# Order of the steps at the seam between attention and experts: shared rows, the first unit's transposes, GpSimd weight sums

## The chip, the cores and the metric

The kernel runs on one core of a Trainium2 chip. The metric is the device time of one execution in microseconds (us); what is compared is the median of several runs. The engines are TensorE (PE in the profile, with its weight loads as PEld), VectorE (DVE), ScalarE (ACT), GpSimd (POOL) and SyncE (SP, which only issues transfers). Each engine works through its own queue in order, and an instruction that waits holds everything behind it.

## The reference, cut to what matters

```python
# attention: batch 8, heads 8, seq 576, head_dim 64; half of the heads see a plain window of 32,
# half a window of 128 with dilation 4
scores = scale * np.matmul(q, k.transpose(0, 1, 3, 2))
scores = np.where(masks[None, :, :, :], scores, -1000000000.0)
attn = softmax(scores)
x = (attn @ v) rearranged to (B, S, H * D)          # 8 x 576 x 512

# experts: 8 of them, w1[e] 512 x 1024, w2[e] 1024 x 512
for b in range(B):
    for s in range(S):
        fresh_e = int(np.argmax(logits[b, s]))
        e = fresh_e if s == 0 or local_gate[b, s] < 0.5 else prev_e
        prev_e = e
        h = np.maximum(x[b, s] @ w1[e], 0.0)
        out[b, s] = p[e] * (h @ w2[e])
```

Each token goes through one expert. Which one depends on its own logits or on the token before it, so the routing is a running scan over the sequence. Everything is computed in float32.

## The kernel before, in words

**Attention.** The 64 heads (8 batches of 8) are worked on two at a time, in 32 pairs. The loop over `n` (lines 1016 to 1044) does `scores(n)`, then `values(n - 1)`, and in every second iteration `turn`, which transposes a finished half of a batch's columns on TensorE, and `store`, which writes it to a buffer in DRAM (`xd`). `load(n + 3)` fetches the keys, queries and values of a later pair through SP's queue. The values tile `vt` has 96 rows for each block of 64 queries: 64 rows of the block and 32 rows that it shares with the block before. The shared rows are copied by GpSimd from the rest of the tile (line 247), directly after the load of the same pair is issued, three iterations ahead of `scores` of that pair.

**Routing.** After every fourth `turn`, `route(g)` puts the routing of 1152 tokens into the list `waiting`: `logits`, `fresh`, `carry`, `carry_over`, `carry_in`, `choose`, `gate`, `place`, `lanes_of`, four `matrices`, `products`, and for groups 1 and 3 `count`, `table` and the tokens. Each step is a few small instructions on TensorE, VectorE and ScalarE. `gap` takes steps from the list in the attention loop by a budget, and `work_gap` takes one after each product of the experts.

**Experts.** The tokens of an expert are gathered into units. A unit of kind "pair" has 256 rows. Units 0 and 1 are chosen early, from the first half of the tokens, while attention still runs. Units 2 and on follow when all tokens are routed. For a unit, `rows_of` gathers rows from `xd` by indirect DMA on GpSimd's queue (line 797); in the attention loop the eight gathers of units 0 and 1 are taken from `rows`, one an iteration, after `load(n + 3)`. `features` transposes them on TensorE (line 812), ScalarE copies them to `xe` (line 813), and VectorE makes four sums `xc` of them.

A pair's two matrix products are each done as seven products of half size instead of eight (`chain`), with sums of the quarters of both operands before and additions after. `hidden(u)` needs `sums[0]`, the four sums of the quarters of w1 (`sums_left`, lines 766 to 769, 128x1024 each), and `xc`. `output(u)` needs `sums[1]`, the four sums of w2 (`sums_right`, lines 772 to 775), and `hc`, four sums of the hidden values (lines 766 to 769 again, 128x512). Product 0 and product 3 use no sums; products 1, 2, 4 and 5 use one left sum each, in order, and products 1, 2, 4 and 6 one right sum. `sums[0]` exists once, so a sum for the next unit can be written when the product that reads the old one is done; so it is with `sums[1]`. In the hidden step VectorE adds a product to an earlier one (line 891), and product 6 waits for the second of these additions. In the output step VectorE does so too (line 965), and `send` writes each half of the unit's rows to the output by indirect DMA on GpSimd's queue (line 909).

TensorE, VectorE and GpSimd execute in the order of the program text. `soon` is a list of sums that `work_gap` puts between products, one or two after each product, and while `waiting` is not empty only when its length is odd. `flush` issues the rest, and `now` issues a list at once. At the seam the order is: hidden step of unit 0 with the w2 sums of unit 0 between; two hc sums; transposes of unit 1; two hc sums and the xc sums of unit 1; output step of unit 0 with the w1 sums of unit 1 between; hidden step of unit 1 with its w2 sums between; four hc sums; output step of unit 1, after whose fourth product `feed` loads weights, transposes unit 2 and gathers unit 3; hidden step of unit 2; transposes of unit 3; w1 sums of unit 3; hidden step of unit 3. From there on the output step of a unit follows the hidden step of the next one.

Of the kernel before, what the change touches and what calls it, by code (L numbers as in the profile page):

```python
# [192 lines left out]
def whole(ctx, tc, exact, bad, qk, v, wgl, w1, w2, con, msk, qmk, out, cst, wg, ones):  # L193
# [50 lines left out]
    def load_values(n):  # L244
        vt = vts[n % AHEAD]
        nc.sync.dma_start(out=vt[WIN:].rearrange("p u i e -> p (u i e)"), in_=v[n])
        nc.gpsimd.tensor_copy(vt[:WIN, :, 1:], vt[QB:, :, :NB - 1])  # L247

    def load(n):
# [134 lines left out]
    def logits(g):  # L384

        st = routes[g]
        xt = st["xt"]
        lp = bank([P, NQ], "lp")
        for kk in range(DK):
            for c in range(NC):  # L390
                if kk < CH:
                    rhs = xt[:, 0, c * NQ:(c + 1) * NQ, kk]
                else:
                    b, s = divmod(c * NQ, S)
                    rhs = xt[:, 1, b * S:(b + 1) * S, kk - CH].rearrange("p (c j) -> p j c", c=DIL)
                    rhs = rhs[:, s // DIL:(s + NQ) // DIL]
                nc.tensor.matmul(lp[c * LW:(c + 1) * LW], lhsT=wg[:, kk], rhs=rhs,
                                 start=(kk == 0), stop=(kk == DK - 1), skip_group_check=True,
                                 tile_position=(0, c * LW))
        st["le"] = le = sm.tile([P, NQ], F32, name="le")  # L400
        nc.scalar.copy(le, lp)
# [332 lines left out]
    def gap(add=None):  # L734
        if add is not None:
            credit[0] = min(credit[0] + add, add)
        alone = False
        while waiting and not alone and (add is None or credit[0] >= 0):
            f, cost, _ = waiting.pop(0)
            credit[0] -= cost  # L740
            if f:
                f()
            alone = add is None or not waiting or waiting[0][2]

    def work_gap(sums=True):
        if waiting:
            gap()
            sums = sums and len(waiting) % 2
        for _ in range(len(soon) > 4 and 2 or len(soon) > 0 if sums else 0):
            soon.pop(0)()  # L750

    def now(push):
        for f in push:
            f()

    def flush():
        while soon:
            soon.pop(0)()

    def quarter(w, i, k, second):  # L760
        if second:
            return w[:, FK // 2 * i:FK // 2 * (i + 1), D // 2 * k:D // 2 * (k + 1)]
        return w[:, FK // 2 * i:FK // 2 * (i + 1), DK // 2 * k:DK // 2 * (k + 1)]

    def sums_left(to, a11, a12, a21, a22):
        return [lambda: nc.vector.tensor_tensor(to[:, 0], a21, a22, op=Alu.add),  # L766
                lambda: nc.vector.tensor_tensor(to[:, 1], to[:, 0], a11, op=Alu.subtract),
                lambda: nc.vector.tensor_tensor(to[:, 2], a11, a21, op=Alu.subtract),
                lambda: nc.vector.tensor_tensor(to[:, 3], a12, to[:, 1], op=Alu.subtract)]

    def sums_right(to, b11, b12, b21, b22):
        return [lambda: nc.vector.tensor_tensor(to[:, 0], b12, b11, op=Alu.subtract),
                lambda: nc.vector.tensor_tensor(to[:, 1], b22, to[:, 0], op=Alu.subtract),
                lambda: nc.vector.tensor_tensor(to[:, 2], b22, b12, op=Alu.subtract),
                lambda: nc.vector.tensor_tensor(to[:, 3], b21, to[:, 1], op=Alu.subtract)]

    def sums_of_weights(u, second):

        i = units[u]["slot"]
        assert (u, second) in loads  # L780
        if second:
            return sums_right(sums[1], *(quarter(raw2[i], k, j, True) for k in range(2) for j in range(2)))
        return sums_left(sums[0], *(quarter(raw1[i], f, k, False) for f in range(2) for k in range(2)))

    xg, xe, xc, ht = {}, {}, {}, {}

# [189 lines left out]
    def route(g, slow):  # L976
        steps = [(logits, 0, True), (fresh, 3.0, True), (carry, 1.0, True), (carry_over, 0.5, True), (carry_in, 0.5, True),
                 (choose, 1.5, True), (gate, 1.5, False), (place, 0.5, True), (lanes_of, 1.3, False)]
        if slow:
            waiting.insert(0, (lambda: logits(g), 0, True))  # L980
            steps.pop(0)
        for f, *how in steps:
            waiting.append((lambda f=f: f(g), *how))
            if slow and f == fresh:
                waiting.append(pause)
        waiting.extend((f, cost, False) for f, cost in zip(matrices(g), (0.9, 0.9, 0.9, 1.7)))
        if g in (EARLY - 1, NG - 1):
            late = g == NG - 1
            counts = count(late)
            steps = [(lambda: next(counts), 1.8, True)] * (PASSES + 1 if exact and late else 2)  # L990
            waiting.append(steps.pop())
            waiting.append((lambda: products(g, False), 0.3, True))
            waiting.extend(steps)
            waiting.append(pause)
            waiting.append((lambda: table(late), 0.3, True))
            if late:
                waiting.append((late_tokens, 1.5, True))
            else:
                waiting.append((early_tokens, 1.5, True))
                waiting.append((early_weights, 0, False))  # L1000
        else:
            waiting.append(pause)
            waiting.append((lambda: products(g, not g), 0.3, True))
# [12 lines left out]
    for n in range(NPB + 2):  # L1016
        if n < NPB:
            (scores_exact if exact else scores)(n)
        gap(SHARE)
        if 1 <= n <= NPB:  # L1020
            values(n - 1)
        if n == NPB - 4:
            soon.extend(sums_of_weights(0, False))
        if soon:
            soon.pop(0)()
        if n >= 3 and n % 2 == 1:
            turn((n - 3) // 2)
            if (n - 3) // 2 % (2 * GB) == 2 * GB - 1:
                route((n - 3) // 2 // (2 * GB), n == NPB + 1)
        gap(SHARE)  # L1030
        if n + 3 < NPB:
            load(n + 3)
        if n >= 3 and n % 2 == 1:
            store((n - 3) // 2)
        if n in (4, 6, 8, 10):
            load_first(0, n // 2 - 2)
        if n == NPB - 4:
            weights(0, True)
            weights(1, False)
        if rows:  # L1040
            rows.pop(0)()
        if n == NPB - 2:
            assert len(rows) <= 4
            now(features(0))
    now(rows)
    attention.close()
    stage = ctx.enter_context(tc.tile_pool(name="late", bufs=1, reuse_waits="tile"))
# [31 lines left out]
    def run_hidden(u, push):  # L1079
        soon.extend(push)  # L1080
        for fits in hidden(u):
            work_gap(fits)
        flush()
        if after[u] is not None and u >= FIRST:
            weights(after[u], False)

    def run_output(u, push):
        soon.extend(push)
        for fits in output(u):
            work_gap(fits)  # L1090
        flush()
        if after[u] is not None and u >= FIRST:
            weights(after[u], True)
# [17 lines left out]
        gather(FIRST + 1)  # L1111

    run_hidden(0, sums_of_weights(0, True))
    first, then = units[0]["sums"][:2], units[0]["sums"][2:]
    now(first)
    then += features(1)
    now(then)
    run_output(0, sums_of_weights(1, False))
    run_hidden(1, sums_of_weights(1, True))
    now(units[1]["sums"])  # L1120
    for k, fits in enumerate(output(1)):
        work_gap(fits)
        if k == FEED:
            feed()
            soon.extend(sums_of_weights(FIRST, False))
    flush()
    weights(after[1], True)
    third = next(u for u in range(NU) if units[u]["slot"] == 2)
    for u in range(FIRST, NU):
        run_hidden(u, both(u - 1) if u > FIRST else [])  # L1130
        if u + 1 < NU:
            now(features(u + 1))
            if u + 2 < NU:
                gather(u + 2)
        push = sums_of_weights(u + 1, False) if is_pair(u + 1) else []
        if u > FIRST:
            run_output(u - 1, push)
        else:
            now(push)
        if units[u]["kind"] == "half":  # L1140
            turned(u)
        if u == FIRST:
            weights(third, False)
            weights(third, True)
        if u in (FIRST + 3, FIRST + 4) and not exact:
            next(checks)
        if u == FIRST + 6 and not exact:
            again = register(bad[0:1, 0:1], 1, "a comparison's result")
# [53 lines left out]
```

## Time and profile before

| what | value |
|---|---|
| runs | 705.75, 708.03, 710.0 us; median 708.03 |
| profiled execution | 706.11 us, of which the span from the first to the last instruction is 703.9 |
| TensorE busy | 671.1 us, 95% of the span |
| VectorE, ScalarE, GpSimd busy | 386.2 (55%), 194.8 (28%), 183.5 (26%) us |
| mean granted clock of TensorE | 0.979 of full speed |
| bytes moved by DMA | 126.59 MB, mean 180 GB/s |
| a w1 or w2 sum on VectorE (128x1024) | 1.22 us |
| the copy of the shared rows on GpSimd (32x1040) | 1.05 us, 32 times |

Busy times overlap between engines and are averages over the whole span. Lines of the profile name the engine, the line of the kernel, the operation, the tile written and the tiles read. In lists of waits, the engine on the left stood idle until the one on the right was done. In timelines, a bracket gives the idle time of the engine just before, and what ended it.

### The profile page before, as it was taken

To read this page: it belongs to the slowest core of one execution; us is meant where nothing else is said; L and a number is where in the kernel's file an instruction comes from. 1 tells how busy PE (TensorE), PEld (TensorE's weight loads), DVE (VectorE), ACT (ScalarE), POOL (GpSimd) and SP (SyncE) were. 2 spreads that over 40 slices of the span, in tenths; PEclk is the share of its full clock that TensorE was granted. 3 is DMA by queue.
4 is the path that set the end of the run, shared out by engine and by line. 5 is a ranking of instruction groups with operands and counts; after the bars stand their busy time and mean duration, and the time that the engine had idled before them with its cause. 6 is when DMAs were issued, how large, how long until landed. Compare 5 with 4: busy or idle time off the path is not lost. (4 is left out here: it accounts for less than half of the span.)

```text
span 703.9 us, 14739 instructions
## 1 busy us (share of the span) xinstructions
PE 671.1 (95%) x6182; PEld 579.1 (82%) x6182; DVE 386.2 (55%) x768; ACT 194.8 (28%) x353; POOL 183.5 (26%) x162
## 2 busy tenths in 40 slices
PE   8999999979997979999999999999999999999994
PEld 6977788756986978999689999599998699996883
DVE  3547478566697558544274572547461828442632
ACT  3544344322311232312122322222222132121220
POOL 3222212230012430402371331513133323032101
PEclk9999999966999999999999999999999999999998
DMA  8999878893102677567262614754004556342201
GB/s 330 321 342 284 250 235 256 257 349 83 73 16 104 226 265 274 184 250 266 84 267 73 229 38 151 245 203 168 31 23 128 217 181 251 135 170 57 122 23 35
DMA packets 38475, 126.59 MB, mean 180 GB/s; under 512 B 4253, under 2 KB 22813, under 8 KB 34432
## 3 DMA queue, kind: packets, MB, share of 16 engines
q1 hardware_dynamic: 31552, 106.15, 43.7%
q0 software_dynamic: 6848, 19.41, 8.0%
q8 instruction: 51, 0.84, 0.5%
q14 instruction: 24, 0.20, 0.1%
HBM read 142.32 MB, written 19.40 MB: 230 GB/s over the span
## 5 line engine op out<-in xcount | busy, mean ns | idle before, releaser
L909 POOL DMA_INDIRECT out_dram<-y,tok x36 | 53.9, 1497 | 323.0 <-DVE y L965 177.5
L881 PE MATMUL hp<-xc,sum 128*128 128x128 f32 x768 | 91.5, 275 | 1.2 <-DVE sum L766 1.2
L950 PE MATMUL yp<-sum,hc 128*128 128x256 f32 x384 | 88.5, 380 | 3.8 <-DVE hc L766 3.4
L881 PEld LDWEIGHTS hp<-xc,sum 128*128 128x128 f32 x768 | 88.5, 192 | 1.4 <-DVE sum L766 1.4
L891 DVE TENSOR_TENSOR h<-hp,h 128x512 f32<-128x512 f32 x48 | 32.9, 689 | 100.1 <-PE hp L881 97.8
L950 PEld LDWEIGHTS yp<-sum,hc 128*128 128x128 f32 x384 | 72.6, 190 | 14.5 <-DVE hc L766 3.4
L881 PE MATMUL hp<-xe,raw 128*128 128x128 f32 x512 | 62.9, 276 | 2.5 <-ACT xe L813 2.5
L881 PEld LDWEIGHTS hp<-xe,raw 128*128 128x128 f32 x512 | 60.2, 192 | 5.2 <-ACT xe L813 2.8
L247 POOL COPY vt<-vt 32x1040 f32<-32x1040 f32 x32 | 34.3, 1073 | 108.0 <-DMA vt<-in_v_dram 86.1
L950 PE MATMUL yp<-raw,h 128*128 128x256 f32 x256 | 60.7, 380 | 0.0
L301 PEld LDWEIGHTS two<-kq 64*96 64x96 f32 x1152 | 53.5, 167 | 7.8 <-issue 7.1
L301 PE MATMUL two<-kq 64*96 64x64 f32 x1152 | 58.0, 254 | 0.0
L965 DVE SCALAR_TENSOR_TENSOR y<-yp,gate,y 128x256 f32<-128x256 f32 x48 | 23.1, 482 | 58.6 <-issue 33.3
L950 PEld LDWEIGHTS yp<-raw,h 128*128 128x128 f32 x256 | 47.3, 190 | 6.1 <-issue 0.4
L797 POOL DMA_INDIRECT xg<-xd,tok x40 | 45.5, 1137 | 23.4 <-PE yp L950 10.6
L306 DVE SCALAR_TENSOR_TENSOR pr<-two,mk 96x512 f32<-96x512 f32 x32 | 21.9, 685 | 52.7 <-ACT pr L308 39.6
L892 ACT ACTIVATE h<-h 128x512 f32<-128x512 f32 x48 | 30.2, 630 | 71.3 <-DVE h L891 64.0
L885 ACT COPY h<-hp 128x512 f32<-128x512 f32 x48 | 28.1, 586 | 74.5 <-PE hp L881 73.3
L797 POOL DMA_INDIRECT xg<-xd,pos x40 | 42.9, 1072 | 12.2 <-issue 11.0
L351 PE MATMUL pv<-vt,pr 96*64 96x65 f32 x1152 | 43.1, 231 | 0.0
L958 ACT ACTIVATE y<-yp,gate 128x256 f32<-128x256 f32 x48 | 22.8, 474 | 66.2 <-PE yp L950 65.1
L351 PEld LDWEIGHTS pv<-vt,pr 96*64 96x64 f32 x1152 | 38.5, 144 | 2.5 <-issue 0.7
(208 smaller groups left out, 1005.1 us busy)
## 6 DMA issues: line engine op xcount, KB each, us to landing
raw<-in_w_dram SPq DMA_DIRECT2D x48, 2048.0 KB
kq<-in_qk_dram SPq DMA_DIRECT2D x32, 592.0 KB
vt<-in_v_dram SPq DMA_DIRECT2D x32, 292.5 KB
xd<-x SPq DMA_DIRECT2D x32, 288.0 KB
raw<-in_w_dram SPq DMA_DIRECT2D x4, 512.0 KB
xg<-xd,tok POOLq DMA_INDIRECT x40
xg<-xd,pos POOLq DMA_INDIRECT x40
out_dram<-y,tok POOLq DMA_INDIRECT x36
```

The source lines that it names most:

```text
L247: nc.gpsimd.tensor_copy(vt[:WIN, :, 1:], vt[QB:, :, :NB - 1])
L301: nc.tensor.matmul(sc[:KW, u, (i - a) * QB:(i - a + 1) * QB], lhsT=kt[h, i * QB:i * QB + KW], rhs=qt[h, i * QB:(i + 1) * QB], start=bool(a ...
L351: nc.tensor.matmul(pv[u * QB:(u + 1) * QB, i - a], lhsT=p[:, u, (i - c) * QB:(i - c + 1) * QB], rhs=vt[:, u, i], start=True, stop=True, ti ...
L797: nc.gpsimd.indirect_dma_start(out=x[:rows, g], out_offset=None, in_=xd[g] if units[u]["late"] else xd[g][:EARLY * GS], in_offset=bass.Ind ...
L881: nc.tensor.matmul(to[:, m], lhsT=a[:, m, kk], rhs=b[:, kk], start=first and m == 0 and kk == 0, stop=(kk == DK // 2 - 1), skip_group_chec ...
L885: nc.scalar.copy(at((0, 1, 3)[k]), of)
L891: nc.vector.tensor_tensor(at(k), of, at(k), op=Alu.add)
L892: nc.scalar.activation(at(k), at(k), Act.Relu)
L909: nc.gpsimd.indirect_dma_start(out=out, out_offset=bass.IndirectOffsetOnAxis(ap=of_unit(u, "tok", j), axis=0), in_=y, in_offset=None, boun ...
L950: nc.tensor.matmul(to, lhsT=a[:, m], rhs=b[:, m], start=first and m == 0, stop=(m == FK // 2 - 1), skip_group_check=True)
L958: nc.scalar.activation(at(k), of, Act.Copy, scale=of_unit(u, "gate", k // 2))
L965: nc.vector.scalar_tensor_tensor(at(k), of, of_unit(u, "gate", k // 2), at(k), Alu.mult, Alu.add)
```

## The change

The copy of the shared rows is split from `load_values` into `share(n)`, called in iteration `n` after `scores(n)`, one iteration ahead of `values(n)`. `features(0)`, after iteration 30 before, is called in iteration 33, ahead of the last `turn`. `logits` of the last group is called at once instead of being put first into `waiting`. The first two hc sums of units 0 and 1 are issued before the rest of `soon`. The w1 and w2 sums of unit 1 are made by GpSimd: the w1 sums are issued after the hidden step of unit 0, the w2 sums after its output step. Two hc sums of unit 0 and the xc sums of unit 1 go into `soon` in the output step of unit 0; two hc sums of unit 1 go into `soon` in its own. The output step of unit 1 is stopped after five products and flushed; its last two products come after the hidden step of unit 2 and the transposes of unit 3, with the w1 sums of unit 3 between and behind. The load of the next second weights of slot 1 follows these.

```diff
     def load_values(n):
         vt = vts[n % AHEAD]
         nc.sync.dma_start(out=vt[WIN:].rearrange("p u i e -> p (u i e)"), in_=v[n])
+
+    def share(n):
+        vt = vts[n % AHEAD]
         nc.gpsimd.tensor_copy(vt[:WIN, :, 1:], vt[QB:, :, :NB - 1])
...
-    def sums_left(to, a11, a12, a21, a22):
-        return [lambda: nc.vector.tensor_tensor(to[:, 0], a21, a22, op=Alu.add),
...
+    def sums_left(to, a11, a12, a21, a22, engine=nc.vector):
+        return [lambda: engine.tensor_tensor(to[:, 0], a21, a22, op=Alu.add),
...
-    def sums_of_weights(u, second):
+    def sums_of_weights(u, second, engine=nc.vector):
...
         if slow:
-            waiting.insert(0, (lambda: logits(g), 0, True))
+            logits(g)
             steps.pop(0)
...
     for n in range(NPB + 2):
         if n < NPB:
             (scores_exact if exact else scores)(n)
+        if n < NPB:
+            share(n)
         gap(SHARE)
...
         if soon:
             soon.pop(0)()
+        if n == NPB + 1:
+            assert len(rows) <= 4
+            now(features(0))
         if n >= 3 and n % 2 == 1:
             turn((n - 3) // 2)
...
         if rows:
             rows.pop(0)()
-        if n == NPB - 2:
-            assert len(rows) <= 4
-            now(features(0))
...
         for fits in hidden(u):
             work_gap(fits)
+        if u < FIRST:
+            now(units[u]["sums"][:2])
         flush()
...
     run_hidden(0, sums_of_weights(0, True))
-    first, then = units[0]["sums"][:2], units[0]["sums"][2:]
-    now(first)
-    then += features(1)
-    now(then)
-    run_output(0, sums_of_weights(1, False))
-    run_hidden(1, sums_of_weights(1, True))
-    now(units[1]["sums"])
-    for k, fits in enumerate(output(1)):
-        work_gap(fits)
+    now(sums_of_weights(1, False, nc.gpsimd))
+    run_output(0, units[0]["sums"][2:] + features(1))
+    now(sums_of_weights(1, True, nc.gpsimd))
+    run_hidden(1, [])
+    soon.extend(units[1]["sums"][2:])
+    rest = output(1)
+    for k in range(FEED + 2):
+        work_gap(next(rest))
         if k == FEED:
             feed()
             soon.extend(sums_of_weights(FIRST, False))
     flush()
-    weights(after[1], True)
...
         if u > FIRST:
             run_output(u - 1, push)
         else:
-            now(push)
+            soon.extend(push)
+            for fits in rest:
+                work_gap(fits)
+            flush()
+            weights(after[1], True)
```

More of the change, by code (lines that the diff above doesn't have):

```diff
@@ L763, in quarter, with sums_right @@
         return w[:, FK // 2 * i:FK // 2 * (i + 1), DK // 2 * k:DK // 2 * (k + 1)]
-    def sums_left(to, a11, a12, a21, a22):
[L766 to L775, printed above, removed]
-    def sums_of_weights(u, second):
+    def sums_left(to, a11, a12, a21, a22, engine=nc.vector):
+        return [lambda: engine.tensor_tensor(to[:, 0], a21, a22, op=Alu.add),
+                lambda: engine.tensor_tensor(to[:, 1], to[:, 0], a11, op=Alu.subtract),
+                lambda: engine.tensor_tensor(to[:, 2], a11, a21, op=Alu.subtract),
+                lambda: engine.tensor_tensor(to[:, 3], a12, to[:, 1], op=Alu.subtract)]
+    def sums_right(to, b11, b12, b21, b22, engine=nc.vector):
+        return [lambda: engine.tensor_tensor(to[:, 0], b12, b11, op=Alu.subtract),
+                lambda: engine.tensor_tensor(to[:, 1], b22, to[:, 0], op=Alu.subtract),
+                lambda: engine.tensor_tensor(to[:, 2], b22, b12, op=Alu.subtract),
+                lambda: engine.tensor_tensor(to[:, 3], b21, to[:, 1], op=Alu.subtract)]
+    def sums_of_weights(u, second, engine=nc.vector):
         i = units[u]["slot"]
@@ L781, in sums_of_weights @@
         if second:
-            return sums_right(sums[1], *(quarter(raw2[i], k, j, True) for k in range(2) for j in range(2)))
-        return sums_left(sums[0], *(quarter(raw1[i], f, k, False) for f in range(2) for k in range(2)))
+            return sums_right(sums[1], *(quarter(raw2[i], k, j, True) for k in range(2) for j in range(2)),
+                              engine)
+        return sums_left(sums[0], *(quarter(raw1[i], f, k, False) for f in range(2) for k in range(2)), engine)
     xg, xe, xc, ht = {}, {}, {}, {}
```

## The prediction

> **What bounds the kernel now.** I read the page first, then TensorE's waits, then the timelines of TensorE, GpSimd and VectorE around each long wait, and the windows of 1 us for the granted clock.
>
> The page: TensorE is busy nearly throughout, and the granted clock falls in one place only.
>
> ```profile
> PE 671.1 (95%) x6182; PEld 579.1 (82%) x6182; DVE 386.2 (55%) x768; ACT 194.8 (28%) x353; POOL 183.5 (26%) x162
> PEclk9999999966999999999999999999999999999998
> ```
>
> From 271 us to 690 us TensorE's timeline shows no wait, so a change of order can win only what is lost before that. TensorE's waits (line that waited, what ended it: total us, times, longest) list nearly all of it:
>
> ```profile
> PE tp L812 <- DMA xg<-xd,tok: 4.2, 1, 4.2
> PE yp L950 <- DVE hc L766: 3.4, 2, 3.0
> PE hp L881 <- ACT xe L813: 2.5, 1, 2.5
> PE hp L881 <- DVE h L891: 2.4, 2, 1.7
> ...
> PE tp L371 <- DVE x L356: 1.8, 1, 1.8
> ...
> PE hp L881 <- DVE sum L766: 1.2, 1, 1.2
> ```
>
> TensorE's timeline (start, us, what, and in brackets the idle time before) places them: the first unit's transposes, the last `turn`, the second unit's output products, the fourth unit's hidden products.
>
> ```profile
> 149.59 1.12 PE L812 MATMUL tp<-cst,xg 128*128 128x128 f32 x4
> 154.92 1.19 PE L812 MATMUL tp<-cst,xg 128*128 128x128 f32 x4 [4.21 <-DMA xg<-xd,tok]
> 155.90 0.74 PE L296 MATMUL two<-mk 96*96 96x320 bf16 x2
> ...
> 168.31 1.30 PE L371 MATMUL tp<-cst,x 128*128 128x128 f32 x9 [1.75 <-DVE x L356]
> 169.54 4.12 PE L397 MATMUL lp<-xt,wg 128*32 128x288 f32 x32
> ```
>
> Why the gather is late, in GpSimd's timeline: it stands in the queue behind a copy that waits for a load.
>
> ```profile
> 139.79 1.01 POOL L797 DMA_INDIRECT xg<-xd,pos  x1 [0.27 <-DVE own L429]
> 147.38 1.04 POOL L247 COPY vt<-vt 32x1040 f32<-32x1040 f32 x1 [6.58 <-PE op L460]
> 148.69 0.96 POOL L797 DMA_INDIRECT xg<-xd,tok  x1 [0.27 <-POOL vt L247]
> ```
>
> **Part 1, shared rows and the first unit's transposes.** `share(n)` stands one iteration ahead of `values(n)`. The load of pair 29 had landed when its copy ran (130.91 us), so with the copies of pairs 30 and 31 (138.47 and 147.38) behind them, the four gathers of unit 0 can follow the tokens (VectorE has them at 128.5) at 1.25 us each, between copies of 1.05: done by about 136, fifteen us before their use. The 32 copies themselves cost nothing more: each runs when its load lands, as now, and `values` uses it an iteration later.
>
> `features(0)` leaves the place before the scores of pair 31. There 149.59 to 155.90, 6.31 us, goes: 2.1 of transposes at half clock and the 4.21. It comes back before the last `turn`, where TensorE idles 1.75 us for VectorE's x. Eight transposes take 0.9 at full clock (0.87 between their starts and the next step's at 315.93 and 316.80) and 1.96 at half (twice 0.98, from 154.92 to 155.90), so at most 0.2 outlasts that wait. Their two ScalarE copies (0.53 each) and four VectorE sums (0.42 each) lie beside `turn` and `logits`, 5.3 us; without that cover the first hidden product would wait about 1 us.
>
> The clock: in the windows it is 0.50 from 145.4 to 165.9 and again from 169.3 to 172.7, after stretches with idle time (142 to 145; 166.6 to 168.3). The second stretch cost `logits` 0.9 (4.12, against 3.23 at 42.84, full clock). Without the idle time it may stay away (-0.6 to -0.9 beyond the 6.31), or the stretch of transposes may be cut to half clock too (`turn` 1.0 longer, transposes outlasting the wait by up to 0.7, sum -4.6). I take -5.7, between. `logits` called at once instead of from the queue changes nothing: it was called in the same place.
>
> **Part 2, weight sums on GpSimd.** Eight sums of 128x1024 (VectorE: 1.22 each, 1.14 in a row). No row shows a two-operand GpSimd instruction. The nearest is its copy of 1040 elements per partition, 1.05 us. Bounds: 1.05, if both operands are read at once; 3.3, if they are read in turn (2.1) and each sum also waits for one VectorE sum (1.22). I take 2.1, the copy once for each operand.
>
> [...]
>
> Do they run beside VectorE? The trace says no:
>
> ```profile
> 112.75 1.50 POOL L247 COPY vt<-vt 32x1040 f32<-32x1040 f32 x1 [3.85 <-DMA vt<-in_v_dram]
> ...
> 138.47 1.04 POOL L247 COPY vt<-vt 32x1040 f32<-32x1040 f32 x1 [5.20 <-DMA xg<-xd,tok]
> ```
>
> ```profile
> 113.26 1.70 DVE L547 TENSOR_TENSOR what<-is_it,gates 96x672 f32<-96x672 f32 x1
> ...
> 138.62 0.92 DVE L425 TENSOR_TENSOR code<-cst,code 96x12 f32<-96x12 f32 x1
> ```
>
> L547 otherwise takes 0.85 and L425 0.17; both end where the copy ends (114.25; 139.51 to 139.54). The copy that took 1.50 had itself waited for the L547 before it. So a GpSimd instruction holds VectorE's work on SBUF operands until it ends, and the two alternate; instructions that read PSUM (L355, L891) are not held. [...] If only the page's 55% for VectorE counted, the sum would be that of the first rival.
>
> First four sums. GpSimd is idle from 155.9 to 204.9 (L909's idle 48.93), so each starts when the product has read its predecessor: 177.3, 181.7, 185.6 and then behind. In times of before: the second (to 183.8) holds `fresh` at L421, 182.79, by 1.0; the third (to 187.7) holds unit 0's L773 by 1.8, which `fresh` had pushed to 185.9; the fourth (188.8 to 190.9) holds L444 by 1.2. L450 on TensorE waits for that and comes at 191.4 instead of 187.57: +3.8. The output step of unit 0 loses its three waits (0.42, 0.26, 0.33), since hc comes before the remaining sums of unit 0 and VectorE no longer has unit 1's: -1.0. Sum +2.8.
>
> Last four. On GpSimd they stand behind two sends; the second send came 4.6 us after the first had ended (208.25, 212.84). Now the second send ends at 214.8; moved by the 2.8, and back by as much for a first send of 1.2 instead of 3.40, the sums run at about 214 to 222.5, over `count` (L576 to L644, some 35 small SBUF instructions, of which one gets in between two sums). VectorE loses 8.4 less the 1.3 it idled, and is spared L768, L769, L772, L773 in the same stretch (4 x 1.14): about 2.5 later at L644. TensorE's L654 waits for that; the waits there before (0.24 and 1.70 for L891) are part of it, so the hidden step of unit 1 is longer by 2.0 (0.5 to 2.5). Behind the sums GpSimd has unit 2's gathers; the tokens that these need come later than the sums end, so the queue costs them nothing.
>
> **Part 3, order around the output step of unit 1.** The wait of 2.98 for hc goes, as the first two hc come at once and no sum of unit 1 is ahead of them. What is late next: unit 2's rows. Its gathers took 225.44 to 231.68 and were used at 233.60 without a wait. TensorE would now be there 4 x 1.73 = 6.9 us after the step's start, the tokens come about 2.0 after it, four gathers take 5.1 and land some 1.6 later: +1.8 (to +4, with the landing time of 4.0 seen at 150.91 to 154.92). After the hidden step of unit 2 two products (3.46) now lie over unit 3's transposes, ScalarE copies and sums: the waits of 2.55 (xe), 1.16 (sum) and 0.74 (h) go. Unit 2's own sums, no longer covered by these two products, cost 0.4. Sum -2.98 - 2.55 - 1.16 - 0.74 + 1.8 + 0.4 = -5.2. The load of unit 3's second weights moves by about 12 us on SP's queue; its first reader is VectorE at 283, about 30 us later: nothing.
>
> **The sum.** -5.7 + 2.8 + 2.0 - 5.2 = -6.1 against the profiled execution (706.11 us, span 703.9): 700.0. The median of the three runs is 708.03, 1.9 above that execution; the forecast for a median is 708.0 - 6.1 = 702 us.
>
> **The rivals.** *No hold (17%).* GpSimd's two-operand sums hardly hold VectorE. For it: gathers beside VectorE's sums took 0.95 to 1.95. Against: the rows above. Then parts 2a and 2b are -1.0 and -1.9, the sum -13.8: 694.
>
> *Slower: GpSimd's sums are long (16%).* One mechanism: each us on a sum is paid about seven times, three times in the chain to L450 and four in that to L654. At 3.3 us (the upper bound) +8.4 gives +2.3, 710; the kernel is slower than before from 3.0 us on, and by over 0.5% from 3.5. At 4 us it is 715. For it: nothing in the trace bounds a two-operand instruction from above but that sum.
>
> *The covered waits stay (22%).* The 2.55 before unit 3's hidden step ended with a release that the profile calls remote, two us after the transposes' modelled end. If the transposes themselves were late, products behind them cannot cover it; and if the clock stays at half as now, part 1 is -4.6. Sum -4.6 + 2.8 + 2.0 - 2.6 = -2.4: 705.6. That the change does not free the gathers at all would need a copy still waiting before them; those ahead of them wait for loads landed by 131, so I give it nothing.
>
> **How the numbers follow.** Forecast 45%, 702, by itself 698 to 706. The range 695 to 710.5 leaves out most of the first rival and the upper half of the second. A measurement of this kernel can tell about 0.5%, 3.5 us, from no change: faster means below 704.5. Faster 0.59 (0.38 of the forecast, 0.17, 0.04 of the third), same 0.25, slower 0.16.
>
> **What would show it.** Right: unit 0's transposes without a wait for xg; TensorE's first hidden product 4.6 to 6.9 us earlier; GpSimd rows of L766 to L775 near 2.1 us; VectorE's small rows in `fresh` and `count` of 2 us beside them; L450 and L654 on TensorE waiting about 4 us each; waits of L950 for hc and of L881 for sum gone; a new wait of L812 of about 2 us for unit 2's rows. Wrong: GpSimd's sums over 3 us, or VectorE's rows unchanged beside them.

## The result: 0.5% slower, and the profile after

The kernel after takes 714.41 us (median of 22 runs, 708.54 to 719.98) beside 709.95 us (22 runs) of the kernel before on the same chip. The ratio is 1.0054, with a 95% interval of 1.0031 to 1.0076: slower by about 3.8 us, where the forecast was faster by 6. The ratio leaves out the few runs that were over 1.5% above the fastest of their kernel, so it is not quite the quotient of the medians. The kernel before, at 706.11 us in its profiled execution, was below its own median; the profiled execution after (714.36 us, span 712.5) is at its median, so the two profiles lie 8.6 us apart and overstate the change.

The page after, TensorE's busy time and its granted clock:

```profile
PE 675.1 (95%) x6182; PEld 583.8 (82%) x6182; DVE 391.1 (55%) x760; ACT 195.1 (27%) x353; POOL 198.5 (28%) x170
...
PEclk9999999978899899999999999999999999999998
```

The number of matmuls is the same, yet TensorE is busy for 4 us more, and the clock now falls in more places, two of them new (slices 11 and 14): the same matmuls ran slower. TensorE's waits (line that waited, what ended it: us, times, longest):

```profile
PE ep L657 <- DVE chosen_late L647: 5.6, 1, 5.6
PE pv L354 <- POOL vt L250: 4.5, 1, 4.5
PE last L453 <- DVE run L447: 4.0, 1, 4.0
PE hp L885 <- ACT h L889: 2.6, 1, 2.6
...
PE tp L816 <- DMA xg<-xd,tok: 1.2, 1, 1.2
```

(Lines have moved by 3 or 4: L247 is now L250, L450 L453, L654 L657, L881 L885.) The waits of before for hc (2.98), for the first unit's rows (4.21) and for sum (1.16) are gone. In their place stand one wait for a copy of the shared rows, which the forecast had at nothing, and two waits for VectorE's routing, for which it had 3.8 and 2.0 us.

**The wait for the copy.** GpSimd's timeline, then TensorE's:

```profile
140.84 1.04 POOL L250 COPY vt<-vt 32x1040 f32<-32x1040 f32 x1 [3.38 <-PE two L304]
142.15 1.77 POOL L801 DMA_INDIRECT xg<-xd,tok  x1 [0.27 <-POOL vt L250]
151.29 1.04 POOL L250 COPY vt<-vt 32x1040 f32<-32x1040 f32 x1 [7.37 <-issue]
152.60 0.98 POOL L801 DMA_INDIRECT xg<-xd,pos  x1 [0.27 <-POOL vt L250]
```

```profile
147.59 0.34 PE L354 MATMUL pv<-vt,pr 96*64 96x65 f32 x4
152.39 2.00 PE L354 MATMUL pv<-vt,pr 96*64 96x65 f32 x32 [4.46 <-POOL vt L250]
```

The load that the copy at 151.29 reads had landed by 132.9. What the copy waited for is the gather ahead of it. In the trace's instruction records each copy behind a gather waits for that gather's semaphore, copies without a gather ahead do not, and the semaphore of the gather at 142.15 got 16 updates, from 148.49 to 151.18. The other four copies behind gathers also start 0.1 to 0.5 us after the last update of the gather ahead of them (134.63, 140.72, 156.50, 161.88). Two copies of before waited in the same way: the one at 138.47 for the gather of 132.24 (last update 138.36), the one at 147.38 for the gather of 139.79 (147.27), though the row of the second names another releaser. They stood three pairs ahead of their reader, and the list of before has no wait of `values` for them; the third gather, behind the second copy, did.

**GpSimd's sums.** All engines, around the first wait; GpSimd's last sum took 3.33 and ended 2.21 us after VectorE's sum (191.20, 188.99), about its own length, so it had itself waited for that:

```profile
185.55 2.36 POOL L771 TENSOR_TENSOR sum<-raw 128x1024 f32<-128x1024 f32 x1 [1.49 <-PE hp L885]
...
186.04 2.95 DVE L776 TENSOR_TENSOR sum<-raw,sum 128x1024 f32<-128x1024 f32 x1
...
187.87 3.33 POOL L772 TENSOR_TENSOR sum<-raw,sum 128x1024 f32<-128x1024 f32 x1
...
189.78 1.62 DVE L447 TENSOR_TENSOR_SCAN run<-row 12x96 f32<-12x96 f32 x1
...
191.46 0.17 PE L453 MATMUL last<-cst,run 12*1 12x12 f32 x1 [4.00 <-DVE run L447]
...
191.56 3.78 PE L885 MATMUL hp<-xc,raw 128*128 128x128 f32 x16
```

The sum of 1.22 took 2.95 and the scan of 0.17 took 1.62; they end 1.08 and 0.20 us after a GpSimd sum does (187.91, 191.20), about their own length. The addition of L895 at 188.91, which reads a product in PSUM, took 0.68 beside the same sum (0.69 in the median). Then comes what the forecast had no term for: hidden product 6 took 3.78 us, against 2.05 before:

```profile
187.57 0.17 PE L450 MATMUL last<-cst,run 12*1 12x12 f32 x1
187.67 2.05 PE L881 MATMUL hp<-xc,raw 128*128 128x128 f32 x16
...
219.17 0.25 PE L654 MATMUL ep<-chosen_late,cst 128*1 128x48 f32 x2 [0.24 <-DVE chosen_late L644]
221.11 2.05 PE L881 MATMUL hp<-xc,raw 128*128 128x128 f32 x16 [1.70 <-DVE h L891]
```

The windows of 1 us of the kernel after say why (the column behind the busy times is the granted clock):

```profile
189.00:190.00 1.00, 0.00 (x0) 0.00 (x0) 0.97 (x3) 0.38 (x1) 1.00 (x1) 1.00 0.00 0
190.00:191.00 1.00, 0.00 (x0) 0.00 (x0) 1.00 (x1) 0.25 (x1) 1.00 (x1) 0.96 0.00 0
191.00:192.00 1.00, 0.54 (x3) 0.51 (x4) 1.00 (x4) 0.00 (x0) 0.20 (x1) 0.50 0.00 0
```

The second wait has the same shape. Four small instructions of `count`, 0.15 to 0.17 us each before, take over 2 us, one beside each GpSimd sum; two of them:

```profile
214.35 2.69 DVE L582 TENSOR_SCALAR ki_late<-ni_late 128x8 int32<-128x8 int32 x1
214.60 2.39 POOL L775 TENSOR_TENSOR sum<-raw 128x1024 f32<-128x1024 f32 x1
...
217.07 2.35 POOL L776 TENSOR_TENSOR sum<-raw,sum 128x1024 f32<-128x1024 f32 x1
...
217.20 2.25 DVE L587 TENSOR_SCALAR ni_late<-ni_late 128x8 int32<-128x8 int32 x1
...
229.58 0.32 PE L657 MATMUL ep<-chosen_late,cst 128*1 128x48 f32 x2 [5.61 <-DVE chosen_late L647]
...
230.39 3.78 PE L885 MATMUL hp<-xc,raw 128*128 128x128 f32 x16 [0.49 <-DVE h L895]
```

### The profile page after: what moved, and what is told of

It is laid out like the page before. It is cut to its first block, busy times and chain, and to the rows that moved or that the text cites. A ratio compares the mean times of both kernels' runs of the same rounds, so it can differ in the third digit from the quotient of the medians.

```text
span 712.5 us, 14756 instructions
## 1 busy us (share of the span) xinstructions
PE 675.1 (95%) x6182; PEld 583.8 (82%) x6182; DVE 391.1 (55%) x760; ACT 195.1 (27%) x353; POOL 198.5 (28%) x170
## 5 line engine op out<-in xcount | busy, mean ns | idle before, releaser
L913 POOL DMA_INDIRECT out_dram<-y,tok x36 | 48.4, 1344 | 291.3 <-DVE y L969 147.3
L885 PE MATMUL hp<-xc,sum 128*128 128x128 f32 x768 | 91.7, 275 | 3.2 <-ACT h L889 2.6
L885 PEld LDWEIGHTS hp<-xc,sum 128*128 128x128 f32 x768 | 88.6, 192 | 3.5 <-ACT h L889 2.8
L895 DVE TENSOR_TENSOR h<-hp,h 128x512 f32<-128x512 f32 x48 | 32.9, 688 | 99.8 <-PE hp L885 97.6
L250 POOL COPY vt<-vt 32x1040 f32<-32x1040 f32 x32 | 34.4, 1075 | 105.7 <-DMA vt<-in_v_dram 62.2
L885 PE MATMUL hp<-xe,raw 128*128 128x128 f32 x512 | 62.8, 276 | 0.0
L885 PEld LDWEIGHTS hp<-xe,raw 128*128 128x128 f32 x512 | 60.3, 192 | 2.5 <-issue 2.1
```

Source lines behind the costliest of these rows:

```text
L885: nc.tensor.matmul(to[:, m], lhsT=a[:, m, kk], rhs=b[:, kk], start=first and m == 0 and kk == 0, stop=(kk == DK // 2 - 1), skip_group_chec ...
L895: nc.vector.tensor_tensor(at(k), of, at(k), op=Alu.add)
L913: nc.gpsimd.indirect_dma_start(out=out, out_offset=bass.IndirectOffsetOnAxis(ap=of_unit(u, "tok", j), axis=0), in_=y, in_offset=None, boun ...
```

## The experiments

Ratios are to the kernel before, run on the same chip, with 95% intervals. From TensorE's timelines two numbers are read for each: H0, the start of the first hidden product of unit 0 (before 173.59, after 173.32), and the seam, from there to the first hidden product of unit 2 (before 66.07, after 73.56).

**share_back.** In the kernel after, the call moves back: `load(n)` ends with `share(n)`, and the loop's `share(n)` goes.

> The changed kernel with the shared rows copied three pairs ahead again; unit 0's transposes stay late. Theory (the copies now wait for the landing of the gather queued before them, and one pair ahead is too short for that): the 4.5 us wait of values(29) for the copy goes, with the slow products after it; the hidden step of unit 0 starts at about 168.5 us instead of 173.3, and the time falls by 4 to 5 us against the changed kernel, to 0.998 to 0.999 of the kernel before. Rival (the late place of unit 0's transposes is worth nothing, and the wait only moves to another step of the attention): the hidden step still starts at 172.5 to 174, and the ratio stays at 1.004 to 1.006.

Measured: 700.63 us, 0.9915 (0.9885 to 0.9945); H0 at 165.23, seam 71.93. No wait for a copy, and a gain about twice the expected one, 9.8 us by the ratios. H0 comes 8.1 us sooner: besides the wait of 4.46, the time at half clock in the attention falls from 17.1 to 6.8 us (in its PEclk line one 8 stands where after has 7 and 8).

**gathers_last.**

```diff
-        if rows:
-            rows.pop(0)()
+        if n >= NPB - 1:
+            now(rows)
+            rows.clear()
```

> The changed kernel with all eight gathers of units 0 and 1 issued after the last copy, in iterations 31 to 33, so that no copy stands behind a gather. Theory: as with the copies three pairs ahead: no wait of TensorE for a copy, the hidden step of unit 0 at about 168.5 us; the gathers go out from about 148 us and have landed by 160, before the transposes of unit 0 at about 162. Time 4 to 5 us below the changed kernel. Rival: the copy isn't the cause, the hidden step starts at 172.5 to 174; or the gathers come too late and the transposes of unit 0 wait 2 us or more for them, and the gain is under 2 us.

Measured: 700.14 us, 0.9890 (0.9850 to 0.9929); H0 at 164.89, seam 71.43. The copies stay one pair ahead, and with no gather in front of them they hold nobody. This takes away what they wait for, and the loss goes.

**sums_vector.**

```diff
-    now(sums_of_weights(1, False, nc.gpsimd))
-    run_output(0, units[0]["sums"][2:] + features(1))
-    now(sums_of_weights(1, True, nc.gpsimd))
-    run_hidden(1, [])
+    now(units[0]["sums"][2:] + features(1))
+    run_output(0, sums_of_weights(1, False))
+    run_hidden(1, sums_of_weights(1, True))
```

> The changed kernel with unit 1's eight weight sums on VectorE again, between the products as in the kernel before (the xc sums of unit 1 and its last two hc sums ahead of the output step again); parts 1 and 3 stay. Theory (the GpSimd sums stop VectorE's small routing instructions, which hold TensorE, and each long wait is followed by products at half clock: 5.3 and 6.3 us in the two stages): the waits for run and for chosen_late fall from 4.0 and 5.6 us to under 1.5 each, from the first hidden product of unit 0 to the first output product of unit 1 it takes about 50 us instead of 61.4, and the time falls by 9 to 12 us against the changed kernel, to 0.988 to 0.993 of the kernel before. Rival (half of it came from the new order of hc and xc sums or from the clock of that run): 4 to 6 us less, a ratio of 0.996 to 1.000.

Measured: 697.40 us, 0.9859 (0.9821 to 0.9897); H0 at 169.44, seam 62.81. The waits for `run` and `chosen_late` fall to nothing and 0.2; from the first hidden product of unit 0 to the first output product of unit 1 it takes 50.7 us.

**filled** and **filled_short.** Dummy matmuls, whose result nobody reads, ahead of the waiting matmuls of the kernel after: `fill(7)` and `fill(10)`, then `fill(4)` and `fill(6)`.

```diff
+    def fill(most):
+        to = bank([P, 512], "fill")
+        for _ in range(most):
+            nc.tensor.matmul(to, lhsT=ident, rhs=cst[:, :512], start=True, stop=True)
...
+        if g == NG - 1:
+            fill(4)
         lp = bank([1, NJ], "last")
...
+        if late:
+            fill(6)
         ep = bank([1, cols], "ep")
```

> The changed kernel with dummy matmuls (128x128 by 128x512) ahead of the two matmuls that wait longest: seven before the one that waits for run, ten before the one that waits for chosen_late, about 3.4 and 4.9 us of otherwise idle time. Theory (the products after the waits are slow because the clock falls after TensorE stood still): hidden product 6 takes 1.95 us in both units instead of 3.78, and with what follows it the time falls by 4 to 6 us against the changed kernel. Rival (they are slow for another reason, such as GpSimd and VectorE on the same memory, or a clock that falls whatever TensorE does): 3.78 us stays, and the time is that of the changed kernel, or up to 1 us above it.

Measured: 707.96 us, 1.0000 (0.9979 to 1.0022); H0 at 170.65, seam 71.71. A dummy took 0.88 us, not 0.49, so the fills lasted 6.2 and 8.8 us and outlasted the waits; product 6 nevertheless ran at full rate (2.05 us).

> The changed kernel again with dummy matmuls ahead of the matmuls that wait for run and for chosen_late, but four and six of them in place of seven and ten, about 3.5 and 5.3 us at the 0.88 us each that filled showed, so that they end before the waits do. Theory (TensorE's standing still lowers the clock): hidden product 6 takes 2.05 us in both units instead of 3.78, the waits end where they did, and it is 4 to 5.5 us less than the changed kernel, a ratio of 0.998 to 1.000. Rival (the gain of filled came from the attention of its runs): 1.003 to 1.006.

Measured: 702.22 us, 0.9938 (0.9903 to 0.9974); H0 at 170.64, seam 67.80. TensorE's timeline:

```profile
184.61 3.60 PE L251 MATMUL fill<-cst 128*128 128x512 f32 x8
188.88 0.17 PE L460 MATMUL last<-cst,run 12*1 12x12 f32 x1 [0.67 <-DVE run L452]
188.97 2.05 PE L894 MATMUL hp<-xc,raw 128*128 128x128 f32 x16
...
218.37 5.32 PE L251 MATMUL fill<-cst 128*128 128x512 f32 x12
224.16 0.24 PE L666 MATMUL ep<-chosen_late,cst 128*1 128x48 f32 x2 [0.47 <-DVE chosen_late L654]
224.97 2.05 PE L894 MATMUL hp<-xc,raw 128*128 128x128 f32 x16 [0.57 <-DVE h L904]
```

Matmuls of no use make the kernel faster: with them the clock stayed at 1.00 from 188 to 191 us, so in the kernel after it fell because TensorE stood still, not because of GpSimd beside it, whose sums are the same: VectorE's `run` and `chosen_late` still came 0.67 and 0.47 us after the fills. Of the gain in the ratio (0.0116, 8 us) the seam shows 5.8, or 4.5 against the mean seam of the four kernels with waits and no fills (after, share_back, gathers_last, share_two); H0, which the edit does not touch, came 2.7 us sooner than in after, and why is open.

**lasts_vector, lasts_w1, lasts_w2.** gathers_last with the edit of sums_vector whole; then with only the w1 sums of unit 1 on GpSimd, and with only the w2 sums.

> Both repairs at once: the gathers of units 0 and 1 after the last copy, and unit 1's weight sums on VectorE. Theory (two separate losses, one in the attention and one in the two hidden steps, which add up): gathers_last gave 0.989 and sums_vector 0.986 where the changed kernel has 1.0054, so 0.989 + 0.986 - 1.005 = 0.970 of the kernel before, with the first hidden product of unit 0 at about 165 us and the hidden step of unit 2 at about 228. Rival (the two share one limit, such as the landing of the second unit's weights, which comes next when TensorE is earlier): 0.978 to 0.985, with a new wait of 3 us or more on TensorE between 165 and 230 us.

> As lasts_vector, but the four w1 sums of unit 1 on GpSimd, behind the hidden step of unit 0. Theory: they hold fresh and the scan behind it on VectorE, TensorE waits 4.0 us for run, and the product after it runs at half clock (1.5 more): 5 to 6 us above lasts_vector, 0.008 of the time. Rival (the first four cost only what was forecast, 2.8 us, and the rest of the measured loss belongs to the last four): 0.003 to 0.005 above lasts_vector.

> As lasts_vector, but the four w2 sums of unit 1 on GpSimd, behind the output step of unit 0. Theory: they hold count on VectorE, TensorE waits 5.6 us for chosen_late, and the product after it runs at half clock: 6 to 7 us above lasts_vector, 0.009 of the time. Rival (as forecast, 2 us, the rest being the first four's): 0.002 to 0.004 above lasts_vector.

Measured: 696.70 us, 0.9818 (0.9779 to 0.9857), seam 61.91; 701.41 us, 0.9911 (0.9882 to 0.9940), seam 65.97; 704.99 us, 0.9955 (0.9926 to 0.9984), seam 67.48. Each half costs by itself: 4.1 and 5.6 us in the seam, 0.009 and 0.014 in the ratio, where 0.008 and 0.009 were expected. lasts_vector lies at the rival's number, not the theory's. Its profile has a new loss, earlier than the rival said and of another kind: in the scores of pair 31, from 151 to 157 us, while the DMA engines were busy all the time (share 1.00 from 150 to 155, 1.04 from 155 to 160), TensorE stopped six times for 4.1 us in all for nothing that the profile shows, and H0 came at 170.14. lasts_w1 and lasts_w2 have such stops too (2.2 and 3.8 us), gathers_last, with the same attention, has none; the cause is open. In lasts_w2, VectorE's rows beside GpSimd's sums, and TensorE's beyond them:

```profile
210.91 2.26 DVE L632 SCALAR_TENSOR_TENSOR to_late<-twice_late,cst,to_late 128x8 f32<-128x8 f32 x1
213.21 2.27 DVE L633 TENSOR_SCALAR twice_late<-nf_late 128x8 f32<-128x8 f32 x1
215.51 2.26 DVE L634 SCALAR_TENSOR_TENSOR to_late<-twice_late,cst,to_late 128x8 f32<-128x8 f32 x1
```

```profile
219.84 0.32 PE L657 MATMUL ep<-chosen_late,cst 128*1 128x48 f32 x2 [6.40 <-DVE chosen_late L647]
220.65 3.78 PE L885 MATMUL hp<-xc,raw 128*128 128x128 f32 x16 [0.49 <-DVE h L895]
```

**part3_alone.** The kernel before with part 3's order alone (the last hunk of the diff and the early hc sums), the rest as in sums_vector and share_back and with unit 0's transposes early.

> The kernel before with part 3 alone: first two hc sums ahead, output step of unit 1 in two parts; the copies, the transposes of unit 0 and the engine of the weight sums are those of before. Theory (the forecast's part 3, -5.2, with a wait of about 1 us for unit 2's rows instead of 1.8): the waits of 2.98 for hc, 2.55 for xe and 1.16 for sum go, 4 to 6 us less than the kernel before, a ratio of 0.992 to 0.994. Rival (the covered waits stay, or belonged to that one profiled run alone): 1.5 to 3 us less, 0.996 to 0.998.

Measured: 702.56 us, 0.9919 (0.9889 to 0.9949); H0 at 173.89, seam 61.93. As the theory has it.

**late_alone** and **share_alone.** The kernel before with one half of part 1 each.

```diff
+        if n == NPB + 1:
+            assert len(rows) <= 4
+            now(features(0))
...
-        if n == NPB - 2:
-            assert len(rows) <= 4
-            now(features(0))
```

> The kernel before, with only the transposes of unit 0 moved behind iteration 32 and logits of the last group called at once; the copies stay three pairs ahead. Theory (this is where all of part 1's gain is, and the split of the copy takes it back): no wait for the rows, the first hidden product at 165 to 166 us instead of 173.6, 7 to 8.5 us less than the kernel before, a ratio of 0.988 to 0.990. Rival (the 8 us between share_back and the two shown profiles belong to the runs, not to the edit; only the forecast's 5.7 or less is there): the first hidden product at 168 us or later, a ratio of 0.992 to 0.996.

> The kernel before, with only the copy of the shared rows moved behind the scores of its own iteration; the transposes of unit 0 stay after iteration 30. Theory (the copies behind the gathers wait for their landing and now hold values): a wait of 4 us or more of TensorE for a copy beside the wait for the rows, the first hidden product at 176 to 181 us, 3 to 8 us slower than before, a ratio of 1.004 to 1.011. Rival (the copies leave the way of the gathers, as the forecast had it, and the rows come sooner): the wait for the rows falls below 2 us and the ratio is 0.994 to 0.999.

Measured: late_alone 697.35 us, 0.9903 (0.9871 to 0.9934), H0 at 163.24; the wait for the rows is 0.6 us, and the clock does not fall in the attention. Its line on the page:

```profile
PEclk9999999999999999999999999999999999999998
```

The line hides one fall in the seam: from 211.67 to 215.09 the clock was at 0.50 (the hidden product at 210.76 took 2.98 us for 2.05), too short to lower the digit of a slice of 17 us. This execution (693.5 us) was the fastest of its six runs, so its H0 flatters the edit; by the ratio the move is worth 6.8 us (4.7 to 9.1).

share_alone 705.18 us, 0.9995 (0.9973 to 1.0018), H0 at 173.68. Neither theory nor rival: TensorE does wait for a copy, but then no longer for the rows.

```profile
152.65 2.00 PE L354 MATMUL pv<-vt,pr 96*64 96x65 f32 x32 [3.85 <-POOL vt L250]
...
156.70 0.69 PE L815 MATMUL tp<-cst,xg 128*128 128x128 f32 x2 [0.40 <-DMA xg<-xd,pos]
```

A gather that lands late is behind both waits. In before it is the second one (139.79 to 147.27): the copy behind it waits for it and holds back the third gather, for which the transposes wait (4.21). With the split it is the third (143.03 to 151.44): `values`, ahead of the transposes, waits for the copy behind it (3.85), and the time stays the same. Move the transposes away as well, as the change does, and the wait stays with `values`. That is where the gain of the move went.

**late_part3.** Copies three pairs ahead, transposes late, part 3, all sums on VectorE.

> The two edits that gain, together: transposes of unit 0 late and part 3, with the copies three pairs ahead and all weight sums on VectorE. Theory (they add): 8 us and 5.5 us less than the kernel before, a ratio of 0.980 to 0.983, the first hidden product of unit 0 at about 165.5 and of unit 2 at about 228 us. Rival (what comes after the first gain takes part of the second, as in lasts_vector): 0.984 to 0.988.

Measured: 692.50 us, 0.9815 (0.9793 to 0.9837), faster than both kernels. The two gains add: 0.9903 and 0.9919 alone. Its one profiled execution took 705.22 us, far above this median, and no H0 is read from it.

**share_two** and **share_two_vector.** The kernel after with the copy two pairs ahead; then also with VectorE's sums.

```diff
-        if n < NPB:
-            share(n)
+        if n == 0:
+            share(0)
+        if n + 1 < NPB:
+            share(n + 1)
```

> The changed kernel with the copy of the shared rows two pairs ahead in place of one; nothing else. Theory (a copy waits for the landing of the gather queued before it, up to 9 us, and one pair of 4.5 us doesn't cover that, two pairs do): no wait of TensorE for a copy of over 0.6 us, the first hidden product at 165 to 167 us, a ratio of 0.991 to 0.996. Rival (the place of the copy isn't what costs, and what share_back gained is from its runs): a first hidden product at 170 us or later, a ratio of 1.002 to 1.006.

> As share_two, and unit 1's weight sums on VectorE. Theory (the two losses are separate): a further 0.010 below share_two, 0.981 to 0.985, as late_part3; the first hidden product at 165 to 167 us and the hidden step of unit 2 at 228 to 230. Rival (the losses overlap, as lasts_vector and gathers_last could mean): within 0.005 of share_two.

Measured: 703.89 us, 0.9989 (0.9960 to 1.0019), H0 at 169.41, seam 72.25; 696.19 us, 0.9861 (0.9814 to 0.9907), H0 at 169.43, seam 65.90. Between theory and rival: two pairs are not enough, since a gather takes up to 9.6 us to land there (142.24 to 151.84; the copy behind it starts at 151.95) and the next one stands right behind the copy.

```profile
153.05 2.00 PE L354 MATMUL pv<-vt,pr 96*64 96x65 f32 x32 [1.37 <-POOL vt L250]
...
160.17 2.00 PE L354 MATMUL pv<-vt,pr 96*64 96x65 f32 x32 [1.68 <-POOL vt L250]
```

With GpSimd's sums, three, two and one pair give 0.9915, 0.9989 and 1.0054: the distance decides. With VectorE's sums the order is weaker (0.9815, 0.9861, 0.9859), and the two losses need not add; with intervals of 0.002 to 0.005 and different chips that is not settled. VectorE's sums are better by 0.010, 0.013 and 0.020 in these three pairs of kernels, and by 0.007 in gathers_last and lasts_vector.

## Why the prediction was wrong, step by step

To the first output product of unit 2 the profiles add up; from there to the end all take 430.4 to 432.9 us.

| part | predicted | measured | from |
|---|---|---|---|
| 1 | -5.7 | -2.7 | H0: mean 171.0 of the four executions with the attention of after (after, sums_vector, filled, filled_short), 173.7 of the two with that of before (before, part3_alone) |
| 2 | +4.8 | +9.9 | H0 to unit 2's first output product: mean 104.1 of four with part 3 and GpSimd sums (after, share_back, gathers_last, share_two), 94.2 of four with VectorE's (sums_vector, lasts_vector, part3_alone, share_two_vector) |
| 3 | -5.2 | -3.6 | the same stretch: those 94.2, against 97.8 of three without part 3 (before, late_alone, share_alone) |
| sum | -6.1 | +3.6 | the ratio says +3.8 |

These sizes are rough. H0 of executions with one and the same attention differs by 3.9 us (169.44 to 173.32 in the four of after) and by 5.2 (164.89 to 170.14 in gathers_last and the three runs built on it), so that the sum comes so near the ratio is in part luck. By the ratios of kernels that differ in one part, each good to about 3 us, part 1 is -4.2 (part3_alone to sums_vector), part 2 is +5, +7, +9 and +14 (the four pairs above) and part 3 is -5.7 and -6.2 (before to part3_alone, late_alone to late_part3). By both, part 2 is the largest miss; by how much parts 1 and 3 fell short, if at all, these sums do not settle. That the copy takes away most of the move's gain rests on share_back, gathers_last and share_alone.

*Part 1: the cause was misread.* The step that failed is "each runs when its load lands, as now", and the sentence that gave no chance to a copy still waiting: the copies wait for gathers. The prediction had the row in its own text, 138.47 with 5.20 behind `DMA xg<-xd,tok`, and took a gather for a load; the copy at 147.38, which it put down to a load as well, waited for a gather too. By the same misreading the gathers were not freed: unit 0's four, which it had done by about 136, went out at 129.68, 136.44, 142.15 and 152.60, and the last of the eight at 166.46, against 154.98 before. The move of the transposes, for which the forecast had taken 5.7, is worth 6.8 and 7.3 us by the ratios where the copies stay three pairs ahead (late_alone against before, late_part3 against part3_alone; H0 of single executions says 8.4 and 10.4, share_back and late_alone). The lower clock in the attention, 20.5 us at 0.50 from 145.39 in before, is 6.8 us in share_back and gone in late_alone.

*Part 2: the hold was right, the clock was left out.* VectorE was held as forecast, with sums of 2.35 us for the 2.1 taken, and L453 waited 4.00 for the 3.8. Without the slow clock (filled_short) the stretch takes 98.9 us, so the hold costs about 4.7, against the 4.8 of the forecast. That these agree is in part luck, by an estimate from the two halves. lasts_w1 and lasts_w2 lose 4.1 and 5.6 us in the seam; TensorE is busy at half clock for 4.8 and 4.4 us there, of which half, 2.4 and 2.2, is lost by an estimate from the granted 0.50. This leaves 1.7 and 3.4 us for the hold, where the forecast had 2.8 and 2.0. The step that failed here is that these waits were priced at their length alone. The missing term is the clock after them, 104.1 - 98.9 = 5.2 by this one execution, of which the two slow products (3.78 for 2.05) account for 3.5. The prediction weighed the clock for part 1 and did not ask what its own new waits would do to it.

*Part 3: mechanism right, one term from a single execution.* The waits for hc (2.98) and sum (1.16) went, and the wait for unit 2's rows came at 1.2 for 1.8. The wait of 2.55 for xe was an event of the one profiled execution: late_alone, with the same order there, has 0.3. After's profile has a like one, 2.62 in unit 2's hidden step, which none but lasts_w1 (1.0) repeats; both ended at 254 to 256 us, behind a ScalarE copy whose own release the profile calls remote, and the cause stays open.

*The rivals.* "No hold" is refuted by the rows of VectorE. "GpSimd's sums are long" had the right sign by the wrong cause: the sums were not long (2.35 us), what they led to was. Its factor, each us paid about seven times, was not tested. "The covered waits stay" did not come about: part3_alone has no wait for xe and 0.4 for sum.

## What to carry to other kernels

Before an instruction is moved nearer to its reader, look up what it waits for, and not only what it reads: by the releaser in the row and, since a row can name another (as at 147.38), by the landing of the transfer queued ahead of it. A wait that its reader did not feel at a distance of three iterations was felt at one (4.46 us). A stall that is taken from one instruction may only pass to the next one behind the same late transfer (here 4.21 us of the transposes, 3.85 of `values`): undo each half alone to see it. A new wait of TensorE of several us is to be priced with the slow matmuls that may follow it (behind 4.00 and 5.61 us here, 3.78 for 2.05), and work given to GpSimd is to be priced by the small VectorE instructions beside it (over 2 us here for 0.15 to 0.17) when TensorE waits for their result.

## What the runs showed of the hardware

The clock: between 100 and 690 us the stretches at 0.50 lasted 20.48 and 3.41 us in before, and 17.07, 6.83 and 6.83 in after, each a whole multiple of 3.41. After the stops of 4.00 and 5.61 us in the seam of after the clock was at 0.50 for 6.83 us each time; behind the stops of 4.00 to 6.40 us in share_back, gathers_last, share_two, lasts_w1 and lasts_w2 hidden product 6 took 3.41 to 3.78 us. The clock fell 3.45 us after TensorE's last matmul in after (187.46 to 190.91), 2.0 in lasts_w1 and 4.5 in lasts_w2. Shorter stops were followed by it in some executions and not in others. In unit 1's hidden step the kernels with VectorE's w2 sums have two stops of 0.24 and 1.70 us with a matmul group of 0.25 between: the clock fell behind them in sums_vector, share_two_vector, late_alone, share_alone and late_part3 (the product behind took 2.65 to 3.68 us), and did not in before, part3_alone, lasts_vector and lasts_w1 (2.05). Before's stop of 2.98 left it at 1.00 (226 to 230). Half clock throughout made 16 matmuls of 2.05 us take 3.78.

How much idle time is enough cannot be read from these runs: in lasts_w1 the clock fell 2.0 us after the stop began, behind two stops of 1.94 us together it fell five times and stayed four times, and in share_two it fell 1.0 us after a stop at 151.68.

GpSimd's sum of 128x1024 took 2.35 us against VectorE's 1.22. In the kernel after a gather took 3.9 to 5.0 us from its start to its semaphore's last update, and 9.0 (142.15 to 151.18) while weights of units 0 and 1 were loading and the DMA engines were busy all the time (0.98 to 1.07 from 144 to 152).
